# A sixth first-layer tile by three products, and other homes for the turned keys, queries and guards

## The chip, the cores and the metric

One core of a Trainium2 chip runs the whole kernel. TensorE (PE) multiplies matrices, and its weight loads are listed apart as PEld. VectorE (DVE) and ScalarE (ACT) work element by element, GpSimd (POOL) issues some DMAs here, and SyncE (SP) issues most of them. Each engine works through its own list of instructions. The metric is the device time of one execution in microseconds (us).

## The reference

A gated linear attention over 768 steps, in 4 batches of 8 heads with 48 columns, and behind it a two-layer network over the 3,072 rows that come out, with the activation h·cos(h):

```python
mag = np.sqrt(a_re * a_re + a_im * a_im)
scale = np.minimum(mag, 0.999) / (mag + 1e-06)
a_re_n, a_im_n = (a_re * scale, a_im * scale)
for t in range(S):
    new_re = ar * S_re - ai * S_im
    new_im = ar * S_im + ai * S_re
    kv = np.einsum('bhd,bhe->bhde', k[:, :, t], v[:, :, t])
    S_re, S_im = (new_re + kv, new_im)
    y[:, :, t] = np.einsum('bhd,bhde->bhe', q[:, :, t], S_re)
x = np.ascontiguousarray(y.transpose(0, 2, 1, 3)).reshape(B * S, H * D)
h = x @ w_in            # 384 -> 2048
g = h * np.cos(h)
return (g @ w_out).astype(np.float32)   # 2048 -> 384
```

## The kernel before

The 3,072 rows are cut into 24 chunks of 128 steps, and two chunks make a group, so there are 12 groups, numbered 0 to 11. Three groups make a batch. Groups 0 and 1 are written out by hand. From group 2 on a loop over n builds three things in one turn: the attention of group n (scores `sc`, the causal mask that gives `atm`, the values `yp`, and the state `sp` carried on), the gates of group n + 1 (logarithms `lg`, exponentials, angles `tan`, then the keys `ks` and queries `qs` with their factors), and the two layers. The second layer of group n − 1 (`op`, `sum`, seven products in place of eight) is threaded through the attention of group n, and the first layer of group n (`hp`) closes the turn. On PE a turn is therefore: scores and values of the group's two chunks between second-layer products, the sums `lgs` and `phs` of the next group's gates, the rest of the second layer, and the first layer. The seam between two turns is where the first layer of group n ends and the scores of group n + 1 start.

The first layer has 8 tiles of 256 columns. A plain tile is six matmuls in full float32, and the profile lists each as two records of 128x256. From a certain group on (table `FROM`) a tile runs by three products instead: x and the weights are cut into an upper and a lower part (`xh`, `xl`, `wh`, `wl`) and a combination of them (`xx`, `wx`), and three times six matmuls in the rounded format give `hp` (two of the products, summed in PSUM) and `hb` (the third). ACT copies `hb` out of PSUM, and DVE adds it to `hp` ahead of the gate. `halves` converts a tile's weights once, at the end of group `FROM` − 1, and `x_halves` cuts x in each group: DVE makes `cut`, `xl`, `xx`, and ACT copies `xh`.

Each gate is a sine and a square on ACT and a product on DVE. Each `hp` takes one PSUM bank, from homes that rotate.

Keys and queries have to stand with their columns on the partitions. `f_transpose` turns them in blocks on DVE (a transpose of 128x1536 into `tr`), SP stores the turned blocks to DRAM (`moved`) and loads them back as `kT` (four loads) and `qT` (one). The attention's output `yT` goes to DRAM and back as `xT` in the same way. SP's list is one queue: a DMA that waits holds the ones behind it.

The weights come as 64-bit numbers. `guard` loads a raw piece again (POOL's DMA) and lets ACT look at its exponents in two passes; two pieces a group, for groups 3 to 10.

The order is set in three ways. PE's list is written out: each matmul is chained behind the one before it, in the order in which `weave` sorts the parts by the numbers beside them. ACT's table functions are chained too. The other rows of DVE and ACT are placed by the framework's scheduler, under the dependencies of tiles and those added by `behind`.

## Time and profile before

| what | us |
|---|---|
| median of three runs | 637.14 |
| lowest and highest of them | 637.04, 642.63 |
| the profiled execution | 635.72 |
| span of its trace, first to last instruction | 633.8 |
| PE idle in this span | 10.4 |
| DVE busy | 530.4 |
| ACT busy | 450.2 |

The span is shorter than the execution by what lies ahead of the first instruction and behind the last. PE's idle time is the span less its busy time of 623.4 us, and nearly half of it is the end, where the last sums are stored. A matmul's duration includes its way through the array, so that records of 0.37 us follow each other in shorter steps: how long a tile takes is read from the starts of the rows. In the rows of the timeline, "x36" is a count of equal records in a row, and what stands in brackets is idle time of the engine ahead of the row and who ended it.

### The profile page before, as it was taken

What the parts mean: (1) busy time and instruction counts of PE and PEld (TensorE: products, weight loads), DVE (VectorE), ACT (ScalarE), POOL (GpSimd) and SP (SyncE); (2) the same over time, 40 slices, a digit from 0 to 9 for tenths busy, and PEclk for the clock granted to TensorE, in tenths of its full rate; (3) what the DMA queues carried; (4) which work ended last, traced back from release to release, by engine and by line L of the source; (5) the groups of instructions that cost most, each with busy time, mean ns of one, the idle gap of its engine ahead of it and who ended that gap; (6) DMA issues with size and microseconds to landing.
All of it is one profiled execution on the core that took longest, in us unless ns stands there. A gap on an engine that the chain in (4) does not pass through costs nothing.

```text
span 633.8 us, 11436 instructions
## 1 busy us (share of the span) xinstructions
PE 623.4 (98%) x4321; PEld 571.4 (90%) x4321; DVE 530.4 (84%) x856; ACT 450.2 (71%) x812; POOL 30.2 (5%) x53
## 2 busy tenths in 40 slices
PE   8999999999999999999999999999999999999996
PEld 6788967677899899999999999999999999999996
DVE  6999989868698799899888998988988988983371
ACT  7888688286597598599598598599598598562350
POOL 4010110000000000000000000000000000000000
PEclk9999999999999999999999999999999999999999
DMA  9968564715926855765865775685675583361001
GB/s 227 254 192 225 177 195 79 199 55 116 243 63 149 215 135 146 180 175 126 201 175 132 180 189 126 172 189 139 177 185 138 162 179 135 111 140 51 26 2 31
DMA packets 232923, 94.94 MB, mean 150 GB/s; under 512 B 208701, under 2 KB 221246, under 8 KB 232858
## 3 DMA queue, kind: packets, MB, share of 16 engines
q1 hardware_dynamic: 225320, 68.51, 47.1%
q0 software_dynamic: 5824, 25.50, 12.1%
q8 instruction: 36, 0.59, 0.4%
q10 hardware_dynamic: 1714, 0.11, 0.2%
q14 instruction: 29, 0.24, 0.1%
HBM read 69.28 MB, written 24.81 MB: 148 GB/s over the span
## 4 chain that ended last, share of the span: by engine, by line
PE 92%; ACT 3%; DVE 3%; issue 1%; DMA 1%; SPq 0%; DVEq 0%
PE hp L692 30%; PE op L692 19%; PE sum L692 16%; PE sc L692 7%; PE yp L692 6%; PE hb L692 5%; PE sp L692 4%; PE phs L692 2%; PE lgs L692 2%; PE yr L692 1%; PE tp L1006 1%; DMA im<-in_a_im_dram 1%; ACT tan L712 1%; DVE tan L681 0%; ACT lg L712 0%
## 5 line engine op out<-in xcount | busy, mean ns | idle before, releaser
L692 PE MATMUL hp<-xT,w_in 128*128 128x256 f32 (+1 forms) x684 | 146.9, 372 | 0.7 <-DVE gate L681 0.7
L692 PEld LDWEIGHTS hp<-xT,w_in 128*128 128x128 f32 x684 | 125.9, 190 | 18.5 <-DVE gate L681 1.1
L692 PE MATMUL op<-w_out,gate 128*128 128x192 f32 (+1 forms) x464 | 103.2, 372 | 0.0
L712 ACT ACTIVATE gate<-hp,half_pi_b 128x512 f32<-128x512 f32 x96 | 65.9, 687 | 43.8 <-PE hp L692 40.4
L692 PEld LDWEIGHTS op<-w_out,gate 128*128 128x128 f32 x464 | 78.7, 190 | 16.7 <-issue 1.9
L681 ACT ACTIVATE junk<-hp 128x512 bf16<-128x512 f32 x96 | 57.2, 596 | 0.0
L692 PE MATMUL sum<-w_out,gate 128*128 128x192 f32 x304 | 54.6, 328 | 0.0
L681 DVE TENSOR_TENSOR gate<-hp,gate 128x512 f32<-128x512 f32 x55 | 37.6, 685 | 18.4 <-ACT junk L681 17.7
L692 PEld LDWEIGHTS sum<-w_out,gate 128*128 128x128 f32 x304 | 49.2, 190 | 0.0
L692 PE MATMUL sc<-qT,kT 96*128 96x128 f32 x384 | 48.9, 276 | 0.3 <-ACT qT L681 0.3
L692 PEld LDWEIGHTS sc<-qT,kT 96*128 96x128 f32 x384 | 46.8, 192 | 2.0 <-issue 0.6
L692 PE MATMUL hp<-xh,wh 128*128 128x256 f32 x246 | 44.2, 288 | 0.0
L692 PE MATMUL hp<-xl,wl 128*128 128x256 f32 x246 | 42.5, 281 | 0.0
L681 DVE TENSOR_TENSOR hp<-hp,gate 128x512 f32<-128x512 f32 x41 | 28.6, 698 | 16.5 <-PE hp L692 7.0
L681 DVE TENSOR_TENSOR atm<-sc,causal 128x512 f32<-128x512 f32 x48 | 32.6, 684 | 7.2 <-PE sc L692 7.2
L681 ACT ACTIVATE ot<-sum 128x192 f32<-128x192 f32 x39 | 12.7, 325 | 34.9 <-PE sum L692 34.9
L681 ACT COPY yT<-yp 48x512 f32<-48x512 f32 x44 | 25.4, 577 | 16.5 <-PE yp L692 16.0
L692 PEld LDWEIGHTS hp<-xh,wh 128*128 128x128 f32 x246 | 35.8, 189 | 0.5
L692 PE MATMUL hb<-xx,wx 128*128 128x256 f32 x246 | 35.1, 284 | 0.0
L681 ACT ACTIVATE gate<-hb 128x512 f32<-128x512 f32 x41 | 24.5, 599 | 14.7 <-PE hb L692 14.0
L692 PEld LDWEIGHTS hp<-xl,wl 128*128 128x128 f32 x246 | 34.8, 188 | 0.0
L681 DVE TENSOR_TENSOR gate<-gate 128x256 f32<-128x256 f32 x80 | 32.2, 417 | 3.0 <-PE op L692 2.5
(163 smaller groups left out, 1275.2 us busy)
## 6 DMA issues: line engine op xcount, KB each, us to landing
moved<-tr SPq DMA_DIRECT2D x20, 768.0 KB
raw<-in_moe_w_in_dram POOLq DMA_DIRECT2D x16, 768.0 KB, 5.5
raw<-in_moe_w_out_dram POOLq DMA_DIRECT2D x16, 768.0 KB, 4.9
kT<-moved SPq DMA_DIRECT2D x40, 192.0 KB
qT<-moved SPq DMA_DIRECT2D x10, 768.0 KB
k<-in_k_dram SPq DMA_DIRECT2D x24, 192.0 KB
q<-in_q_dram SPq DMA_DIRECT2D x24, 192.0 KB
v<-in_v_dram SPq DMA_DIRECT2D x24, 192.0 KB
```

What stands on the lines that cost most here:

```text
L681: ins = getattr(self.engine, op)(**kw)
L692: chain(nc.tensor.matmul(out, **kw), "tensor")
L712: chain(nc.scalar.activation(func=func, **kw))
L1006: chain(nc.tensor.transpose(ps[:, h], X[g][name[0] + "s"][:, x0 + h].rearrange("p a d -> p (a d)"), ident), "tensor")
```

## The change

It has five parts.

1. `FROM` gets a sixth tile, 2, from group 5 on, and tiles 3 and 6 start one group earlier. Tiles by three products: 2 before and 3 now in group 3, 4 and 5 in group 4, 5 and 6 from group 5 on, that is 41 and 50 in all. The conversions lie in groups 2 (three), 3 (two) and 4 (one), in place of two, two and one.
2. The turned keys lie in `kT`'s own home and the turned queries in `qT`'s, ahead of the loads that fill these. Before, they had the home `tr` and the home of `pair`.
3. The guards' raw pieces, which had `tr`'s home, lie in the homes of `kT` and `qT` too, once the attention of the group has read these. Their places in the turn are 0.47 and 0.505 instead of 0.26 and 0.47, and the small copy on POOL that held them back is gone.
4. x is halved between the two turns. `cut` comes behind the keys' turn, `xl` and `xx` follow, and the queries' turn is placed behind `xx`. Before, both turns came first.
5. The store of x goes ahead of the load of `im` in SP's queue. And `hp` rotates over four banks from group 2 on, in place of three.

```diff
-    def guard(src):
-        _, e = fetched(src)
+    def guard(src, home):
+        _, e = fetched(src, home)
...
     def f_transpose(g, i, n, name):
-        if i == 0:
-            X[g][name] = ft.tile([D2, G * H, Q4, 32] if name == "kT" else [D2, Q4, G * H, 32], F32,
-                                 tag=name, name=name, bufs=1)
-        pool, tag = (ft, "tr") if name == "kT" else (gt, "pair")
-        tr = pool.tile([C, NB, n * H, 32], F32, tag=tag, name="tr", bufs=1)
+        tr = ft.tile([C, NB, n * H, 32], F32, tag=name, name="tr", bufs=1)
...
         X[g][name + " turn"] = turn
+        if g and name == AHEAD and "apart" in X[g - 1]:
+            behind(turn, X[g - 1]["apart"])
...
+        X[g][name] = ft.tile([D2, G * H, Q4, 32] if name == "kT" else [D2, Q4, G * H, 32], F32,
+                             tag=name, name=name, bufs=1)
...
-            home = "mmc"[len(order) % 3] if g != 1 else "a"
+            home = "a" if g == 1 else "mamc"[len(order) % 4] if g else "mmc"[len(order) % 3]
...
-            vector.tensor_scalar(out=x["cut"].bitcast(U32), in0=whole.bitcast(U32), scalar1=UPPER,
-                                 scalar2=None, op0=ALU.bitwise_and)
+            cut_ = vector.tensor_scalar(out=x["cut"].bitcast(U32), in0=whole.bitcast(U32), scalar1=UPPER,
+                                        scalar2=None, op0=ALU.bitwise_and)
+            if g + 1 < NG:
+                behind(cut_, X[g + 1][BEFORE])
...
-            copied = scalar.copy(out=x["xh"], in_=x["cut"])
-            if g + 1 < NG:
-                behind(copied, x["square"])
-            low = vector.tensor_tensor(out=x["xl"], in0=all_of(), in1=x["cut"], op=ALU.subtract)
-            if g + 1 < NG:
-                behind(low, X[g + 1]["qT turn"])
-                behind(low, x["product"])
+            scalar.copy(out=x["xh"], in_=x["cut"])
+            vector.tensor_tensor(out=x["xl"], in0=all_of(), in1=x["cut"], op=ALU.subtract)
...
+        if "apart" in x and g + 1 < NG and jp == x["order"][0]:
+            behind(gated, x["apart"])
...
-    FROM, UPPER, SHIFT = {3: 5, 4: 3, 5: 3, 6: 4, 7: 4}, 0xFFFFF000, 4096.0
+    FROM, UPPER, SHIFT = {2: 5, 3: 4, 4: 3, 5: 3, 6: 3, 7: 4}, 0xFFFFF000, 4096.0
+    BEFORE, AHEAD = "kT turn", "qT"
...
-            yield lambda: load(g + 1, ("re", "im"))
+            yield lambda: load(g + 1, ("re",))
...
-        yield lambda: (f_x(g), f_xt(g))
+        yield lambda: (f_x(g), g + 2 < NG and load(g + 2, ("im",), put=after_x), f_xt(g))
...
-              (convert[0:1], 0.82, 0.82), (convert[1:2], 0.93, 0.93),
+              (convert[0:-2], 0.76, 0.76), (convert[-2:], 0.76, 0.98),
```

In the lists of the engines this shows at three places, all taken from the turn that ends at the seam of 370.66 us in the trace of before. The first is DVE behind the gates, where keys and queries are turned and x is halved (`end` is a small step of the state). Before:

```order
L681 STREAM_TRANSPOSE tr_3182<-ks_3165 128x1536
L681 STREAM_TRANSPOSE tr_3203<-qs_3166 128x1536
L681 TENSOR_SCALAR cut_3171<-xT_3081 128x768
L681 TENSOR_TENSOR gate_3197<-hp_3190,gate_3197 128x512
L681 TENSOR_TENSOR xl_3169<-xT_3081,cut_3171 128x768
L681 SCALAR_TENSOR_TENSOR xx_3168<-xl_3169,cut_3171 128x768
L681 TENSOR_SCALAR end_3063<-end_3063 96x16
```

The same place on DVE now:

```order
L681 STREAM_TRANSPOSE tr_3224<-ks_3213 128x1536
L681 TENSOR_SCALAR cut_3236<-xT_3125 128x768
L681 TENSOR_TENSOR xl_3234<-xT_3125,cut_3236 128x768
L681 SCALAR_TENSOR_TENSOR xx_3233<-xl_3234,cut_3236 128x768
L681 TENSOR_TENSOR gate_3248<-hp_3241,gate_3248 128x512
L681 STREAM_TRANSPOSE tr_3253<-qs_3214 128x1536
L681 TENSOR_SCALAR end_3101<-end_3101 96x16
```

The three steps of x and the first gate have moved ahead of the queries' turn.

The second place is SP's queue behind the turns: the stores of the turned blocks (`moved`), the loads of `kT` and `qT`, and what stands behind them. Before:

```order
L990 DMA moved_3184<-tr_3182 128x1536
L990 DMA moved_3205<-tr_3203 128x1536
L994 DMA kT_3181<-moved_3184 96x16x32 x4
L996 DMA qT_3202<-moved_3205 96x4x512
L1488 DMA out_0_dram<-ot_2939 128x384
L1488 DMA out_0_dram<-ot_2938 128x384
L1488 DMA k_3210<-in_k_dram 128x8x48 x2
```

SP's queue at the same place now:

```order
L988 DMA moved_3226<-tr_3224 128x1536
L994 DMA kT_3228<-moved_3226 96x16x32 x4
L988 DMA moved_3255<-tr_3253 128x1536
L996 DMA qT_3257<-moved_3255 96x4x512
L1493 DMA out_0_dram<-ot_2988 128x384
L1493 DMA out_0_dram<-ot_2987 128x384
L1493 DMA k_3261<-in_k_dram 128x8x48 x2
```

The four loads of `kT` now stand ahead of the store of the queries.

The third place is DVE at the seam: the masks `atm` of the first chunk's scores, the logarithm steps of the next gates (`lg`, `pair`), the last gates, and the mixes of gates for the second layer (`s`, and `gate` from gates). Before:

```order
L681 TENSOR_TENSOR atm_3405<-sc_3406,causal_165 128x512
L681 TENSOR_TENSOR lg_3378<-lg_3378,tan_3379 128x768
L681 TENSOR_TENSOR s_3412<-gate_3240,gate_3342 128x256
L681 SCALAR_TENSOR_TENSOR gate_3371<-hp_3351,gate_3371 128x512
L681 TENSOR_TENSOR atm_3405<-sc_3421,causal_165 128x512
L681 TENSOR_TENSOR s_3427<-gate_3265,gate_3371 128x256
L681 SCALAR_TENSOR_TENSOR state_3439<-sp_3430,state_3018 96x384
L681 TENSOR_TENSOR gate_3240<-gate_3240 128x2x128
L681 TENSOR_TENSOR state_3439<-state_3439,end_3063 96x384
L681 SCALAR_TENSOR_TENSOR pair_3381<-re_3031,pair_3381 128x768
L681 TENSOR_SCALAR lg_3378<-lg_3378 128x768
```

DVE at the same seam now:

```order
L681 TENSOR_TENSOR lg_3441<-lg_3441,tan_3442 128x768
L681 TENSOR_TENSOR gate_3301<-gate_3301 128x2x128
L681 SCALAR_TENSOR_TENSOR gate_3434<-hp_3414,gate_3434 128x512
L681 TENSOR_TENSOR s_3490<-gate_3324,gate_3434 128x256
L681 TENSOR_TENSOR gate_3324<-gate_3324 128x2x128
L681 SCALAR_TENSOR_TENSOR pair_3444<-re_3075,pair_3444 128x768
L681 TENSOR_SCALAR lg_3441<-lg_3441 128x768
L681 TENSOR_TENSOR atm_3468<-sc_3469,causal_165 128x512
L681 TENSOR_TENSOR lg_3441<-lg_3441,rs_3443 128x768
L681 TENSOR_TENSOR gate_3248<-s_3412,gate_3248 128x2x128
L681 TENSOR_TENSOR gate_3276<-s_3452,gate_3276 128x2x128
L681 TENSOR_TENSOR atm_3468<-sc_3484,causal_165 128x512
```

The first mask has moved from ahead of the logarithm steps to behind `pair` and `lg<-lg`, and the second to behind `lg<-lg,rs`. The seams ahead of groups 6 to 10 have this form now, two of them (groups 6 and 9) with one mix fewer ahead of the second mask. At the seam ahead of group 4 the first mask stands ahead of `pair` and the second behind `lg<-lg,rs`; at that of group 5 the second mask stands right behind `lg<-lg`; at those of groups 3 and 11 both stand ahead of these steps. PE's list is the same as before, but for the nine tiles.

More of the change, by code (lines that the diff above doesn't have):

```diff
@@ L1509, in wait_for, with guarded @@
         chain(nc.gpsimd.tensor_copy(out=after, in_=tile), "gpsimd")
-    def guarded(g, count):
-        if guards:
-            yield lambda: wait_for(X[g]["gate"][X[g]["order"][-1]][0:1, 0, 0:1])
-        for _ in range(min(count, len(guards))):
-            yield lambda: guard(guards.pop(0))
+    def guarded(homes):
+        for home, _ in zip(homes, list(guards)):
+            yield lambda home=home: guard(guards.pop(0), home)
     into, back = weight_parts()
     guards = [src for _, src in into + back if src.dtype != F32]
-    per = -(-len(guards) // (NG - 3))
     after = consts.tile([1, 1], F32, name="after")
@@ L1800, in fast_path @@
         split = x_halves(n) if any(three(n, jp) for jp in THREE) else ()
-        guard_ = list(guarded(n - 1, per)) if n > 2 else []
+        guard_ = list(guarded(("kT", "qT"))) if n > 2 else []
         convert = [lambda jp=jp: halves(jp) for jp in THREE if FROM[jp] == n + 1]
-        if split and n < NG - 1:
-            X[n + 1]["upper"] = split[0]
         weave((mixes(n - 1, 2, 4), 0.0, 0.08), (logs(n + 1), 0.0, 0.02), (chunks(n), 0.0, 0.36),
```

24 lines of the change are left out of this document (14 added, 10 removed).

## Prediction

> **What bounds the kernel now.** I read the page's busy times first, then the windows by loop turn, and then the timelines of PE, DVE, ACT and SP around one seam between two turns of the loop over groups (all rows that follow show the start and the duration in us).
>
> The page, then two windows (busy time of PE, PEld, DVE, ACT and POOL, granted clock, DMA share, GB/s):
>
> ```profile
> PE 623.4 (98%) x4321; PEld 571.4 (90%) x4321; DVE 530.4 (84%) x856; ACT 450.2 (71%) x812; POOL 30.2 (5%) x53
> ...
> 322.40:370.70 48.30, 48.30 (x363) 46.43 (x362) 42.99 (x69) 37.65 (x70) 1.67 (x3) 1.00 0.67 164
> 630.00:634.00 4.00, 0.00 (x0) 0.00 (x0) 0.00 (x0) 0.00 (x0) 0.00 (x0) 0.71 0.12 35
> ```
>
> PE sets the time: in a turn of 48.3 us it is busy for all 48.3. A shorter matmul stream is a direct gain, but every new wait of PE is a direct loss, since PE has no idle time to take it from. DVE, at 43.0 of 48.3 us, is the engine that can make PE wait.
>
> One seam on PE (start, duration): the end of the first layer of one group, then the chunks of the next.
>
> ```profile
> 352.19 7.93 PE L692 MATMUL hp<-xT,w_in 128*128 128x256 f32 x36
> 359.77 0.70 PE L692 MATMUL hp<-xh,wh 128*128 128x256 f32 x3
> ...
> 367.09 0.52 PE L692 MATMUL hp<-xh,wh 128*128 128x256 f32 x3
> ...
> 369.23 0.51 PE L692 MATMUL hp<-xh,wh 128*128 128x256 f32 x3
> ...
> 370.66 1.05 PE L692 MATMUL sc<-qT,kT 96*128 96x128 f32 x8
> ...
> 375.06 1.53 PE L692 MATMUL sum<-w_out,gate 128*128 128x192 f32 x8
> 376.52 0.43 PE L692 MATMUL yp<-atm,v 128*48 128x128 f32 x4
> ...
> 377.44 0.39 PE L692 MATMUL yp<-atm,v 128*48 128x128 f32 x4
> ...
> 378.42 1.57 PE L692 MATMUL op<-w_out,gate 128*128 128x192 f32 x8
> ```
>
> Call 370.66, where the scores `sc` start, the seam's zero. The values `yp` of the first chunk start at 5.86; their first four heads need the first mask `atm`, the last four (377.44, at 6.78) the second. The same seam on DVE and ACT:
>
> ```profile
> 372.13 0.68 DVE L681 TENSOR_TENSOR atm<-sc,causal 128x512 f32<-128x512 f32 x1
> 372.74 0.96 DVE L681 TENSOR_TENSOR lg<-lg,tan 128x768 f32<-128x768 f32 x1
> ...
> 374.55 0.68 DVE L681 TENSOR_TENSOR atm<-sc,causal 128x512 f32<-128x512 f32 x1
> ...
> 377.02 0.96 DVE L681 SCALAR_TENSOR_TENSOR pair<-re,pair 128x768 f32<-128x768 f32 x1 [0.19 <-ACT pair L712]
> 377.89 0.55 DVE L681 TENSOR_SCALAR lg<-lg 128x768 f32<-128x768 f32 x1
> 378.36 0.42 DVE L681 TENSOR_TENSOR gate<-gate 128x256 f32<-128x256 f32 x1
> 378.79 0.96 DVE L681 TENSOR_TENSOR lg<-lg,rs 128x768 f32<-128x768 f32 x1
> 379.67 1.08 DVE L681 TENSOR_TENSOR gate<-s,gate 128x256 f32<-128x256 f32 x3
> ...
> 373.88 1.28 ACT L708 ACT_TABLE_LOAD   x1
> ...
> 376.89 0.83 ACT L712 ACTIVATE rs<-lg 128x768 f32<-128x768 f32 x1
> ...
> 377.84 0.93 ACT L712 ACTIVATE rs<-rs,one_b 128x768 f32<-128x768 f32 x1
> ```
>
> Both masks are done at 375.23, 1.3 us before `yp`. The logarithm steps come after them: `pair` waits for ACT's exponential, which stands behind the last gate and a table load of 1.28 us. In this order that wait (0.19 us) costs nothing.
>
> **The sixth tile.** A plain tile takes 12 records: three of them take 359.77 − 352.19 = 7.58 us, so 2.53 each. A tile by three products takes 369.23 − 367.09 = 2.14. The first such tile costs 0.18 more (0.70 against 0.52), as before. Nine tiles change form (one in group 3, one in group 4, one in each of groups 5 to 11): 9 × 0.39 = 3.5 us off PE. What the form adds beside PE, per tile one more ACT step out of PSUM and one DVE sum, lies in the first layer, where both engines wait for PE. The one conversion more (now three in group 2) lies beside plain tiles of 2.53 us. I cost both at nothing; where ACT falls behind, the logarithms of the seam come later, up to about one step (0.8 us) a seam.
>
> **The fourth home for `hp`.** In group 2, PE waits once for a bank:
>
> ```profile
> 162.01 13.22 PE L692 MATMUL hp<-xT,w_in 128*128 128x256 f32 x60 [0.67 <-DVE gate L681]
> ```
>
> With four homes the fifth tile needs the first gate later, so 0.7 us goes. Sum so far: −4.2.
>
> **Halving x between the turns.** The turns of keys and queries on DVE, the halving of x behind them, and SP's queue after the turns:
>
> ```profile
> 353.67 2.25 DVE L681 STREAM_TRANSPOSE tr<-ks 128x1536 f32<-128x1536 f32 x1
> 355.86 2.20 DVE L681 STREAM_TRANSPOSE tr<-qs 128x1536 f32<-128x1536 f32 x1
> 357.98 0.52 DVE L681 TENSOR_SCALAR cut<-xT 128x768 uint32<-128x768 uint32 x1
> ...
> 359.02 0.94 DVE L681 TENSOR_TENSOR xl<-xT,cut 128x768 fp32r<-128x768 f32 x1
> 359.99 0.96 DVE L681 SCALAR_TENSOR_TENSOR xx<-xl,cut 128x768 fp32r<-128x768 f32 x1
> ...
> 354.98 0.69 ACT L712 ACTIVATE gate<-hp,half_pi_b 128x512 f32<-128x512 f32 x1 [2.26 <-PE hp L692]
> ...
> 358.58 0.83 ACT L681 CAST xh<-cut 128x768 fp32r<-128x768 f32 x1 [2.33 <-DVE cut L681]
> ...
> 355.95 2.48 SPq L990 DMA_DIRECT2D moved<-tr  x2
> 359.16 4.20 SPq L994 DMA_DIRECT2D kT<-moved  x4
> 363.47 1.10 SPq L996 DMA_DIRECT2D qT<-moved  x1
> ```
>
> The tiles by three products now start after two plain ones, at 352.19 + 5.06 = 357.25. The keys' turn frees DVE at 355.9 (the queries' turn starts 2.19 after it); `cut`, `xl`, `xx` then end near 356.4, 357.3 and 358.2. The copy `xh` on ACT (0.83) can be there at about 357.2, just in time; `xl` is needed three matmuls, `xx` twelve matmuls later. I take 0, with 0.3 us a turn (some 2 us in all) as the upper end.
>
> **Turned keys, queries and guards.** The guards' two passes on ACT keep one place and take another in the 2.3 us in which ACT waits for the first tile, so nothing; if they landed late, the keys' turn on DVE, and all behind it, would wait for them. SP now issues the keys' four loads ahead of the queries' store. Before, store to landing took at most 359.16 − 355.95 = 3.2 us, and `qT` had 370.66 − 363.47 = 7.2 us to land. Now: loads until 363.4, store 3.2, and at most 7.2 for the load, so 373.8 at the latest against scores wanted at 370.3. The likely landing is near 370, as the store alone took 3.2 for the same bytes. Scores later by up to 3.5 us are covered where the masks are later still (next part), and cost up to 3.5 us elsewhere. I take 0. `x` ahead of `im` brings xT earlier; PE does not wait for xT now, so 0.
>
> **The masks' place on DVE.** This decides. As the order in the section on the change shows, at this seam the two masks now stand behind `pair` and `lg<-lg`, and the second also behind `lg<-lg,rs` and two mixes. The chain on ACT does not move: it hangs on the last gate. So DVE reaches the first mask at 378.36 (where the mix stood) and ends it at 379.04; `lg<-lg,rs` from 378.97 takes 0.88, two mixes 0.34 each, and the second mask runs from 380.52 to 381.20. `yp` starts 2.5 us late, and its second half at 381.25 instead of 377.44: 3.8 us. All that PE has after it shifts; the second chunk's masks fit under the shifted work (by my count to within 0.3 us), and nothing later in the turn had idle time to give back. Where the change puts one mix fewer ahead of the second mask, the first chunk of a batch is at hand, whose halves are shorter:
>
> ```profile
> 328.28 1.08 PE L692 MATMUL yp<-atm,v 128*48 128x128 f32 x16
> 330.55 0.96 DVE L681 TENSOR_TENSOR lg<-lg,rs 128x768 f32<-128x768 f32 x1
> ...
> 231.72 0.39 PE L692 MATMUL yp<-atm,v 128*48 128x128 f32 x4
> 235.09 0.96 DVE L681 TENSOR_TENSOR lg<-lg,rs 128x768 f32<-128x768 f32 x1
> ...
> 281.60 0.39 PE L692 MATMUL yp<-atm,v 128*48 128x128 f32 x4
> 282.76 0.55 DVE L681 TENSOR_SCALAR lg<-lg 128x768 f32<-128x768 f32 x1
> ```
>
> There the first mask again goes ahead of `lg<-lg,rs`: 330.7 + 0.88 + 0.34 + 0.68 = 332.6 against the second half at 328.8, so 3.8 too. Five seams (chunks of groups 6 to 10) have these forms: 19. At group 4's only the second mask is behind: 235.09 + 0.88 + 0.68 = 236.65 against 231.72, so 4.9. At group 5's it is behind `lg<-lg` alone: 282.76 + 0.47 + 0.68 = 283.9 against 281.60, so 2.3. Groups 3 and 11 have both masks ahead of such waits: 0.2 at most. Sum: 19 + 4.9 + 2.3 + 0.2 = 26.4.
>
> The seam leaves PE idle for 2.5 and then 1.3 us, at group 4's for 4.9 at one stretch. In the profile the clock is 1.00 in all turns, and 0.71 in the last four microseconds, with PE idle. The Trainium skill (TensorE: Matmul & The Clock Gate, section "What's actually happening", the table of the two states) says that a whole idle window of about 3.4 us halves the clock until PE has been busy for another such window. By it the sum would, as an estimate, be 1.7 us longer, for the one gap that can hold a window; the last row fits it, and no gap before that is long enough to test it.
>
> **Sum.** 26.4 − 4.2 = +22.2 us on the profiled execution's 635.7, so 657.9. The median of the runs, 637.14, is 1.4 above that execution; on it the sum is 659.3. I say 659.
>
> **Rivals.**
> 1. Not slower: PE doesn't lose at the masks, because something else ends the wait, or the work after `yp` catches up. What speaks for it is only that nothing waits there now. Then the gain stands alone: 637.1 − 4.2 = 632.9, 0.7% down. It decides if `yp` starts under 0.5 us late at each of seven seams. Against it: DVE's rows of the trace stand in the order of the program. Chance 0.06.
> 2. The queries land late as well: up to 3.5 us at the seams that the masks don't cover (group 11, 3.5; group 3, whose turns are earlier, some 2; group 5, 1.2): +6.7, so 666. Chance 0.12.
> 3. Only the first mask counts, since ACT's chain or the mixes are quicker: 2.5 instead of 3.8 at five seams, so 653. Chance 0.08.
> 4. The clock falls in each of the seven gaps: at half clock the rest of `yp` (377.44 to 378.42) and the `op` behind it (1.57) cost up to 2.6 us more, so up to 18 in all, 677. Every gap but one is split by half a `yp`. Chance 0.06.
>
> **How the numbers follow.** The forecast has 0.68, the rivals 0.32. The range 651 to 668 takes in the forecast, rival 2 and rival 3 with the 2 us of `xh`, which makes 0.86, less some 0.05 for what I don't see. One per cent is about what a measurement here can tell from no change: faster by over 1% means under 630.8, below even rival 1, so 0.01; within 1%, 0.05; slower, 0.94.
>
> **What would show it.** Right: PE rows of `yp<-atm` in groups 6 to 10 with an idle time before them released by DVE's `atm`, about 2.5 and 1.3 us; PE's idle time up by 26; `hp<-xT` down by 108 records, each of the three product groups up by 54. Wrong: no such idle time, or `sc` waiting for a DMA, or a clock below 1.00 in these windows.

## The result, and the profile after

| what | before | after |
|---|---|---|
| median, us | 637.64 | 692.40 |
| lowest and highest, us | 637.04, 642.63 | 690.92, 695.37 |
| the profiled execution, us | 635.72 | 690.92 |
| span of its trace, us | 633.8 | 689.1 |
| PE busy, us | 623.4 | 639.8 |
| PE idle in the span, us | 10.4 | 49.3 |
| mean granted clock of PE | 0.998 | 0.965 |

The changed kernel is slower by 8.5%: the ratio is 1.0846, with a 95% interval of 1.0779 to 1.0913. The prediction had the direction. Its time of 659.0 and its range up to 668 fell short.

The span grew by 55.3 us, in two parts that the table shows. PE is idle for 38.9 us more. And it is busy for 16.4 us more, although nine tiles went to the shorter form (3.5 us less by the prediction's rows): some 19.9 us are matmuls at a lower clock.

PE's waits after (total us, how many, the longest), the costliest first:

```profile
PE sc L692 <- DMA qT<-moved: 17.6, 4, 4.8
PE sum L692 <- DVE gate L681: 10.5, 4, 4.3
PE sc L692 <- issue: 5.5, 2, 4.5
PE sc L692 <- ACT tan L756: 3.7, 1, 3.7
PE sc L692 <- ACT junk L681: 3.1, 1, 3.1
```

Four of these rows are one thing. The scores wait at eight of the nine seams from group 3 on, 29.9 us in all. Where the row names that load, the wait ends 5.9 to 6.3 us after its issue; where the row names ACT or nothing, it ends 5.9 to 7.0 us after it, so it is taken for the same wait. The other row is new in kind: `sum`, the first product of the second layer, waits for a gate of the first layer.

One steady seam on PE (the one ahead of group 7): start of the first layer, its end, and the chunk behind it.

```profile
375.36 5.34 PE L692 MATMUL hp<-xT,w_in 128*128 128x256 f32 x24
...
393.02 0.52 PE L692 MATMUL hp<-xl,wl 128*128 128x256 f32 x3
398.27 2.05 PE L692 MATMUL sc<-qT,kT 96*128 96x128 f32 x8 [4.73 <-DMA qT<-moved]
400.11 2.77 PE L692 MATMUL sum<-w_out,gate 128*128 128x192 f32 x8
...
406.42 0.43 PE L692 MATMUL yp<-atm,v 128*48 128x128 f32 x4
```

Before, eight score records took 1.05 us and eight of `sum` 1.53; here 2.05 and 2.77. The first values `yp` start 8.15 us after the scores, not 5.86: 2.3 us go to the clock, on top of 4.73 of waiting. `yp` itself doesn't wait, so the masks, on which the prediction rested, cost nothing here. The clock in three stretches of this seam (column PEclk, the third from the end):

```profile
393.00:398.20 5.20, 0.54 (x5) 0.34 (x3) 5.03 (x11) 5.17 (x10) 0.00 (x0) 0.79 0.89 234
398.20:401.50 3.30, 3.23 (x13) 3.26 (x14) 1.99 (x4) 3.24 (x5) 0.00 (x0) 0.50 1.14 225
401.50:405.00 3.50, 3.50 (x30) 3.50 (x28) 3.00 (x6) 3.00 (x5) 0.00 (x0) 0.81 0.02 4
```

And the queue of SP ahead of this seam:

```profile
379.11 0.34 SPq L988 DMA_DIRECT2D moved<-tr  x1
382.44 4.10 SPq L994 DMA_DIRECT2D kT<-moved  x4
386.63 2.36 SPq L988 DMA_DIRECT2D moved<-tr  x1
392.35 0.33 SPq L996 DMA_DIRECT2D qT<-moved  x1
```

On DVE, the queries' turn, for which the second store waits:

```profile
382.03 2.29 DVE L681 STREAM_TRANSPOSE tr<-qs 128x1536 f32<-128x1536 f32 x1
```

The queries' turn ends at 384.32, but SP is still issuing the keys' loads, so the store goes out at 386.63. From there to the load's issue pass 5.7 us (3.2 in the prediction), and from that issue to the scores 5.9. This order of the queue holds at seven of the nine seams, ahead of groups 5 to 11; from the store to the load's issue it is 4.3 to 5.7 us there, so the seam shown is the longest.

### The profile page after: what moved, and what is told of

It reads as the page before. It is cut to its first block, busy times and chain, and to the rows that moved or that the text cites. A ratio compares the mean times of both kernels' runs of the same rounds, so it can differ in the third digit from the quotient of the medians.

```text
span 689.1 us, 11622 instructions
## 1 busy us (share of the span) xinstructions
PE 639.8 (93%) x4375; PEld 588.8 (85%) x4375; DVE 543.5 (79%) x868; ACT 457.7 (66%) x823; POOL 28.3 (4%) x45
## 4 chain that ended last, share of the span: by engine, by line
PE 76%; DVE 8%; ACT 7%; DMA 6%; issue 2%; SPq 0%; ACTq 0%; DVEq 0%
PE hp L692 18%; PE op L692 18%; PE sum L692 16%; PE sc L692 7%; PE yp L692 6%; PE sp L692 4%; DMA qT<-moved 3%; PE hb L692 2%; PE phs L692 2%; ACT gate L712 2%; DVE gate L681 2%; DVE tr L681 2%; DMA moved<-tr 2%; ACT junk L681 1%; PE lgs L692 1%
## 5 line engine op out<-in xcount | busy, mean ns | idle before, releaser
L692 PE MATMUL hp<-xT,w_in 128*128 128x256 f32 (+1 forms) x576 | 123.1, 371 | 0.0
L692 PEld LDWEIGHTS hp<-xT,w_in 128*128 128x128 f32 x576 | 105.6, 190 | 14.7 <-issue 0.2
L692 PEld LDWEIGHTS sc<-qT,kT 96*128 96x128 f32 x384 | 53.8, 215 | 33.1 <-issue 20.5
L692 PE MATMUL sum<-w_out,gate 128*128 128x192 f32 x304 | 67.0, 378 | 10.5 <-DVE gate L681 10.5
L692 PEld LDWEIGHTS sum<-w_out,gate 128*128 128x128 f32 x304 | 60.1, 225 | 11.2 <-issue 10.4
L692 PE MATMUL hp<-xh,wh 128*128 128x256 f32 x300 | 53.2, 286 | 0.0
L692 PE MATMUL hp<-xl,wl 128*128 128x256 f32 x300 | 51.7, 281 | 0.0
L692 PEld LDWEIGHTS hp<-xh,wh 128*128 128x128 f32 x300 | 43.2, 189 | 0.9 <-ACT xh L681 0.5
L692 PE MATMUL hb<-xx,wx 128*128 128x256 f32 x300 | 42.8, 283 | 0.0
L692 PEld LDWEIGHTS hp<-xl,wl 128*128 128x128 f32 x300 | 42.5, 188 | 0.0
L681 DVE SCALAR_TENSOR_TENSOR gate<-hp,gate 128x512 f32<-128x512 f32 x50 | 34.3, 686 | 8.8 <-ACT junk L681 8.7
```

Source lines behind the costliest of these rows:

```text
L681: ins = getattr(self.engine, op)(**kw)
L692: chain(nc.tensor.matmul(out, **kw), "tensor")
```

## The experiments

Fifteen kernels ran in five groups, each beside runs of the kernel before, whose medians there were 636.7 to 637.2. Times below are medians, and the ratio to before stands with its interval.

### The homes of `hp`

The first group set two theories of the trace against the prediction's masks. The fourth home: the rotation "mamc" puts the eighth tile into c, the one bank of the tag `acc`, which the next turn's `sum` takes too. The queue: the queries land late. The changed kernel with three homes again:

```diff
-            home = "a" if g == 1 else "mamc"[len(order) % 4] if g else "mmc"[len(order) % 3]
+            home = "a" if g == 1 else "mmc"[len(order) % 3]
```

> The changed kernel with the three homes of before for hp, all else as changed. Three theories are on trial. Queue: the queries' store stands behind the keys' four loads in SP's queue, so the queries land 4 to 5 us late, and PE's clock falls in the gap. Home: with four homes the eighth tile lies in the bank that the next group's sum takes, so sum waits for the last gate. Masks: what the prediction said. The home theory expects the waits of sum for gate (10.5 us in four of them, in the seams ahead of groups 3, 4 and 5 and at the end) to go to below 1 us, and the time to fall by about 10, to some 682. The queue theory alone expects the waits of sc in the steady seams to stay at 4 to 5 us each, whatever the homes. If the home were behind the late scores too (they take banks of the same pool as the fourth home), those waits would go as well, and the time would be near 655.

Measured: 665.65, ratio 1.0452 (1.0432 to 1.0473), 27 us below the changed kernel rather than 10. `sum` no longer waits at all. The scores wait 15.4 us in all instead of 29.9, and a wait of `hp` for the first gate appears:

```profile
PE sc L692 <- ACT gate L712: 7.6, 3, 2.7
PE hp L692 <- DVE gate L681: 7.0, 8, 1.4
PE sc L692 <- ACT junk L681: 4.7, 2, 2.8
PE sc L692 <- DMA qT<-moved: 3.1, 2, 1.6
```

The kernel before with the fourth home alone:

```diff
-            home = "mmc"[len(order) % 3] if g != 1 else "a"
+            home = "a" if g == 1 else "mamc"[len(order) % 4] if g else "mmc"[len(order) % 3]
```

> The kernel before with the fourth home for hp alone (four homes in the order of the change from group 2 on). Home: sum waits for the last gate at every seam, by up to 3 us, so 10 to 30 us longer than before, 648 to 668. The prediction's term (0.7 us shorter): 637. Queue: no effect on the queries, no wait of sc for a DMA.

Measured: 688.59, ratio 1.0829 (1.0771 to 1.0886). This one line takes the kernel before to almost the time of the whole change, and beyond the 648 to 668 that I had expected of it. The first row of its waits, then one seam on PE and on DVE:

```profile
PE sum L692 <- DVE gate L681: 30.9, 10, 5.0
```

```profile
394.44 1.05 PE L692 MATMUL sc<-qT,kT 96*128 96x128 f32 x8
398.82 2.19 PE L692 MATMUL sum<-w_out,gate 128*128 128x192 f32 x8 [3.33 <-DVE gate L681]
```

```profile
397.99 0.68 DVE L681 SCALAR_TENSOR_TENSOR gate<-hp,gate 128x512 f32<-128x512 f32 x1
```

The scores start at once, since the queries are on time. Then `sum` starts 0.15 us after the end of the last gate (397.99 + 0.68 = 398.67): that product is the last reader of the eighth tile, and it stands behind the whole chain of the tile on ACT and DVE. Of the 49.5 us that the span grew (683.3 against 633.8), 30.9 are this wait and 18.9 are PE's busy time (642.3 against 623.4), that is the clock.

To see whether a fourth home or its place is at fault, the changed kernel with the banks in another order, so that the third tile lies in c:

```diff
-            home = "a" if g == 1 else "mamc"[len(order) % 4] if g else "mmc"[len(order) % 3]
+            home = "a" if g == 1 else "macmmamm"[len(order)] if g else "mmc"[len(order) % 3]
```

> The changed kernel with another rotation of the four kinds of bank: the first layer's tiles lie in m, a, c, m, m, a, m, m, so that the bank of sum (c) holds the third tile and is free long before the seam. Home: no wait of sum for a gate (below 1 us in all), as with three homes, and no wait of hp for a gate either (6.3 us in the steady turns with three homes). Queue: the queries land when they did, so what hp no longer waits for is added to the wait of sc, 2.5 to 4.7 us at each of seven seams, and the time is 655 to 670, near the one with three homes. If the queries were late only because hp waited, or the home were the only fault, the time would be 633.

Measured: 668.27, ratio 1.0469 (1.0425 to 1.0513), as expected of the two theories together. Neither `sum` nor `hp` waits. The scores wait 23.8 us (the rows of `sc` summed), up to 3.6 at a seam. The two costliest of these rows:

```profile
PE sc L692 <- DMA qT<-moved: 12.6, 4, 3.6
PE sc L692 <- ACT junk L681: 6.4, 2, 3.2
```

So it is the place: the same number of banks, 24 us less. And what the bank gave back to `hp` (7.0 us) went to the wait of the scores.

A run with one line changed can differ from its neighbour in more than that line. The lists of SP and DVE aren't written out as PE's is, and they moved with the homes. In the two runs with other homes (665.65 and 668.27) both stores stand ahead of the keys' loads, and on DVE the queries' turn stands ahead of the first gate, at all seams from group 6 on but the last. SP in the run at 668.27, ahead of group 7:

```profile
364.79 4.99 SPq L988 DMA_DIRECT2D moved<-tr  x2
369.95 6.34 SPq L994 DMA_DIRECT2D kT<-moved  x4
```

The gain of 24 us is therefore that of the bank together with these orders. That the bank by itself makes `sum` wait is what the run at 688.59 shows.

### The late queries

The order of SP's queue was the first suspect. The changed kernel with the keys' loads behind the queries' store, as before:

```diff
         if name == "kT":
-            for q4 in range(Q4):
-                nc.sync.dma_start(out=X[g][name][:, ds(i * H, n * H), q4], in_=moved[q4])
+            X[g]["kT loads"] = [(X[g][name][:, ds(i * H, n * H), q4], moved[q4]) for q4 in range(Q4)]
         else:
+            for home, src in X[g].pop("kT loads"):
+                behind(nc.sync.dma_start(out=home, in_=src), put)
             late["qT"] = nc.sync.dma_start(out=X[g][name][:, :, ds(i * H, n * H)],
```

> The changed kernel with the keys' four loads issued behind the queries' store, the order of SP's queue before; the turns on DVE and all else stay as changed. Queue: the queries' store lands 3.2 us after its issue in place of 5.7, the queries' load is issued some 3 us earlier, the scores wait about 2 us at a steady seam instead of 4 to 5, the gap is below 3.4 us and the clock of PE stays at full speed (eight score records in 1.05 us, not 2.05): 7 seams with 2.5 to 3 less of waiting and 2.3 less of slow matmuls, so some 36 us less, near 657. Masks: as soon as the queries are on time, the waits of yp for atm appear (2.5 and 1.3 us a seam), and the time stays above 670. Home: the waits of sum for gate stay (10.5) and appear at the steady seams also, up to 3 us each.

Measured: 697.83, ratio 1.0937 (1.0908 to 1.0966): no gain. The queries are as late as in the changed kernel, only for another reason:

```profile
383.09 4.99 SPq L988 DMA_DIRECT2D moved<-tr  x2
388.24 6.38 SPq L996 DMA_DIRECT2D kT<-moved  x4
394.79 0.96 SPq L997 DMA_DIRECT2D qT<-moved  x1
```

```profile
402.02 2.05 PE L692 MATMUL sc<-qT,kT 96*128 96x128 f32 x8 [4.51 <-DMA qT<-moved]
```

The keys' turn ends at 383.06. Its loads could start some 3 us later, but stand behind a store that waits for the queries' turn (385.40 to 387.70). The theory in its first form, that the order in the list is the fault, fell. What stays is that the queries' turn comes late, and that one list then has two orders to choose from, both bad. This run has the order that the two runs with other homes got by themselves, and the queries' load goes out as late as in the run at 668.27, some 15.4 us after the start of the first layer.

The changed kernel with both turns first, the halving of x behind them:

```diff
-    BEFORE, AHEAD = "kT turn", "qT"
+    BEFORE, AHEAD = "qT turn", None
...
-              (split[0:1], *[0.57 if n < NG - 1 else 0.525] * 2),
+              (split[0:1], *[0.601 if n < NG - 1 else 0.525] * 2),
```

(and 0.602 and 0.603 for the other two steps). Once with the homes of the change, once with those of the last run:

> The changed kernel with both turns ahead of the halving of x, as before, so that SP's queue has its order of before; six tiles by three products, four homes, and all else as changed. Queue: no late queries (waits of sc below 1 us in all), but the first tile by three products starts after two plain tiles, before xh is there: about 2.2 us a turn in seven turns, 15 in all. With the home's waits of 10 to 30 us the time would be 660 to 680; without them (home theory wrong) some 650. Masks: yp waits for atm by 2 to 4 us a seam on top of that.

> The changed kernel with both turns ahead of the halving of x and with the rotation m, a, c, m, m, a, m, m; six tiles. Home and queue: no wait of sum for a gate, none of sc for the queries; only the first tile by three products waits for xh, 2.0 to 2.5 us in each of six turns (12.8 in all with the four homes of the change), so 637 - 4 + 13 = 646. Sixth tile as a cost of its own (its added steps on ACT and DVE): 655 or more. Masks: where they stand behind the logarithms on DVE, 2.6 and 0.3 us of waiting for each such seam come on top.

With "mamc": 708.02, ratio 1.1102 (1.1059 to 1.1146). The queries are on time, so the whole price of the bank shows: `sum` waits 33.1 us, `hp` waits 12.8 for `xh`. That is beyond what I expected, since the clock falls at most seams as well. With the other homes: 646.25, ratio 1.0154 (1.0139 to 1.0168), which is what the sum gave. Nearly all that is left is the wait for `xh` (`yp` waits 0.8 us for masks, `sc` 0.7):

```profile
PE hp L692 <- ACT xh L681: 11.0, 6, 2.5
```

The sixth tile thus has its price on either side: with two plain tiles ahead, x is halved either too late for PE (11.0 us) or ahead of the queries' turn.

What the halving between the turns costs without a sixth tile and without a fourth home:

```diff
-    FROM, UPPER, SHIFT = {2: 5, 3: 4, 4: 3, 5: 3, 6: 3, 7: 4}, 0xFFFFF000, 4096.0
+    FROM, UPPER, SHIFT = {3: 5, 4: 3, 5: 3, 6: 4, 7: 4}, 0xFFFFF000, 4096.0
...
+            home = "a" if g == 1 else "mmc"[len(order) % 3]
```

> The changed kernel with the five tiles by three products and the three homes of before; x is still halved between the turns of keys and queries. Queue: the sixth tile only shortens the first layer by 0.4 us a turn, so the scores still wait for the queries at the steady seams, about 2 us each, with the clock falling at some: 650 to 660. If the sixth tile's shorter first layer (or its added steps on ACT and DVE) is what makes the queries late, the time is that of before, 637.

> As the run with five tiles and three homes, but with both turns ahead of the halving of x: what is left of the change are the turned keys, queries and guards in the homes of kT and qT, the store of x ahead of im, and the places of the conversions. Queue and home: nothing of it costs, 636 to 639, no wait of PE of over 1 us in the loop. If the homes of the turned blocks or the guards delay the turns, the scores wait for the queries here too, 645 or more.

Halving between the turns: 657.43, ratio 1.0313 (1.0274 to 1.0352). Both turns first: 646.58, ratio 1.0146 (1.0114 to 1.0178). The 11 us between them are late queries: the scores wait 7.7 us in the one and not in the other, and at the last seam the clock falls too. In both runs `hp` waits for the first gate, 8.3 and 8.8 us. The waits of the first:

```profile
PE hp L692 <- DVE gate L681: 8.3, 8, 1.5
PE sc L692 <- ACT junk L681: 3.6, 2, 2.9
PE sc L692 <- DMA qT<-moved: 2.7, 4, 1.0
...
PE sc L692 <- issue: 1.4, 1, 1.4
```

The second run isn't the kernel before in time, as I had expected. Its 9.4 us are the wait of `hp`: with three homes the fourth tile takes the first tile's bank and waits for that tile's gate, and this gate had become late. Two places could make it so. On ACT, the copy `xh` stood ahead of the gate's sine; on DVE, `xx` stood ahead of the gate's product. Two lines that the change drops had kept these apart. One came back first, then both:

```diff
-            scalar.copy(out=x["xh"], in_=x["cut"])
-            vector.tensor_tensor(out=x["xl"], in0=all_of(), in1=x["cut"], op=ALU.subtract)
+            copied = scalar.copy(out=x["xh"], in_=x["cut"])
+            if g + 1 < NG:
+                behind(copied, x["square"])
+            low = vector.tensor_tensor(out=x["xl"], in0=all_of(), in1=x["cut"], op=ALU.subtract)
+            if g + 1 < NG:
+                behind(low, x["product"])
```

(the first of the two runs without the last two lines and `low`).

> The run with five tiles, three homes and both turns first (646.6) had hp wait 8.8 us for the first gate. In its trace ACT's copy xh stands ahead of the first gate and waits about 5 us for cut, which stands behind the turns on DVE. Here the line that the change drops is back: xh is held behind the first tile's square. If this place of the copy is the cause, the wait of hp falls to 0.7 us (the one in group 2) and the time to that of before, 637. If the first gate is late for another reason (its place on DVE behind xx), hp still waits over 5 us and the time stays at 645 or more.

> The last run with five tiles, three homes and both turns first, with the second line that the change drops back as well: xl is held behind the first tile's product on DVE, so that the first gate stands ahead of xl and xx again. If this place on DVE is what makes hp wait (in the run without it the sine on ACT is done some 5 us before the product starts, which stands behind xx), the waits of hp fall from 8.9 us to 0.7 and the time to 637, that of the kernel before. If they stay, the cause is elsewhere, and the time stays at 646.

With the line on ACT: 646.56, ratio 1.0156 (1.0136 to 1.0176), no change. With both: 637.11, ratio 1.0018 (0.9987 to 1.0049), the time of before. The first of these on ACT and on DVE:

```profile
359.33 0.69 ACT L712 ACTIVATE gate<-hp,half_pi_b 128x512 f32<-128x512 f32 x1 [1.46 <-PE hp L692]
```

```profile
363.93 0.96 DVE L681 SCALAR_TENSOR_TENSOR xx<-xl,cut 128x768 fp32r<-128x768 f32 x1
...
365.09 1.88 DVE L681 TENSOR_TENSOR gate<-hp,gate 128x512 f32<-128x512 f32 x3
```

The sine is done at 360.0, and the product starts 5.1 us later, behind `xx`. That is the place. In the change this price is hidden by the fourth home, which lets the fourth tile start without that gate.

Last, the queries' store from ACT's list, with the homes of the run at 668.27, so that in SP's queue no store that waits for the queries' turn holds back the keys' loads:

```diff
-        put = nc.sync.dma_start(out=moved.rearrange("q (r b) x j -> (q r) b x j", b=NB), in_=tr)
+        queue = nc.scalar if name == "qT" and g > PEG + 1 else nc.sync
+        put = queue.dma_start(out=moved.rearrange("q (r b) x j -> (q r) b x j", b=NB), in_=tr)
```

> The changed kernel with the rotation m, a, c, m, m, a, m, m, and the queries' store issued from ACT's list in place of SP's, so that it neither stands behind the keys' four loads nor they behind it. Queue, in its first form (the order in SP's list makes the queries late): the queries' load is issued some 2.5 us earlier, the wait of sc falls from 2.7 to 3.6 to about 1 us a seam, below what lowers the clock, and the time falls from 668 to some 645. Second form (the transfers themselves, above all the keys' loads in pieces of 128 bytes, keep the DMA engines busy, so the queries land late in any order once their turn comes 2.4 us later): no gain, 660 to 670.

Measured: 648.53, ratio 1.0203 (1.0158 to 1.0247): 20 us less than with the store in SP's list. The store leaves 0.03 us after the turn, and the load follows 4.6 us later:

```profile
362.39 2.29 DVE L681 STREAM_TRANSPOSE tr<-qs 128x1536 f32<-128x1536 f32 x1
...
364.71 0.33 ACTq L989 DMA_DIRECT2D moved<-tr  x1
...
369.33 0.71 SPq L997 DMA_DIRECT2D qT<-moved  x1
```

So one queue for both was the larger part of the delay. The rest is the later turn: seven waits of `sc` of 0.6 to 2.0 are left (8.7 us), and ACT, which now waits for the turn itself ahead of the first gate, makes `hp` wait 4.4 us.

The same with `xh` behind the first square again, and the steps of x emitted behind the first tile (places 0.59, 0.592 and 0.594):

> The run with the queries' store on ACT's list (648.5) with the same line back, so that the first gate goes ahead of xh; the steps of x are emitted behind the first tile. Six tiles, homes m, a, c, m, m, a, m, m. If hp's 4.4 us of waiting only move to the scores, which wait for the queries anyway, the time stays at 644 to 649. If the earlier gates also let the queries' turn and its store go earlier, it falls to 640 or below, and with the 4.2 us of shorter matmuls it could come under the kernel before.

Measured: 660.03, ratio 1.0361 (1.0331 to 1.0391), worse. `hp` waits 13.3 us for `xh` in three turns, up to 5.4 at once. In the one shown the store stands ahead of the first gate and of `xh` in ACT's list, and ACT does nothing for 7.4 us: the store goes out at 370.08, when the queries' turn on DVE has ended (370.05). The row names `least`, a small step of DVE right behind that turn:

```profile
370.08 0.33 ACTq L989 DMA_DIRECT2D moved<-tr  x1
370.45 0.69 ACT L712 ACTIVATE gate<-hp,half_pi_b 128x512 f32<-128x512 f32 x1 [7.36 <-DVE least L681]
...
371.61 0.83 ACT L681 CAST xh<-cut 128x768 fp32r<-128x768 f32 x1
```

Whether the waits of `hp` and of `sc` are in parallel this run doesn't tell; a store that waits for its data holds what stands behind it in its list, the gates on ACT as the keys' loads on SP.

The seam ahead of group 7 in five kernels, in us from the start of that turn's first layer:

| kernel | queries' turn ends | their load is issued | scores start |
|---|---|---|---|
| before | 5.9 | 11.3 | 18.5 |
| changed | 9.0 | 17.0 | 22.9 |
| five tiles, three homes | 8.4 | 13.6 | 21.2 |
| six tiles, homes m, a, c, m, m, a, m, m | 8.4 | 15.4 | 21.7 |
| the same, store from ACT's list | 8.4 | 13.0 | 20.0 |

### The clock

The changed kernel with ten matmuls that nobody reads in the gap, ahead of the scores of groups 6 to 11:

```diff
-        return [lambda jp=jp: mm1(g, jp, jp == order[-1]) for jp in order]
+        return [lambda jp=jp: (mm1(g, jp, jp == order[-1]),
+                               jp == order[-1] and 4 < g < NG - 1 and fill(10)) for jp in order]
+
+    def fill(count):
+        ps = pa.tile([C, 512], F32, tag="a", name="busy")
+        for _ in range(count):
+            matmul(ps[:, 0:E2], lhsT=w_out[:, 0, 0:C], rhs=w_out[:, 1, 0:E2],
+                   start=True, stop=True)
```

> The changed kernel with ten matmuls of 128x192 (some 3.3 us, their result is read by nobody) on PE behind the last first-layer tile of groups 5 to 10, where PE otherwise waits for the queries. Clock: PE is busy through most of the gap, so the first eight score records take 1.05 to 1.15 us again in place of 2.05, and the eight of sum 1.5 in place of 2.8, some 2.2 us at each of six seams: 679. If the slow matmuls behind the gap have another cause (the transfers that run beside them, say), they stay slow and the time stays at 692 or grows.

Measured: 674.87, ratio 1.0602 (1.0581 to 1.0624): 17.5 us shorter than the changed kernel, by adding work. The same seam:

```profile
389.05 3.41 PE L692 MATMUL busy<-w_out 128*128 128x192 f32 x20
393.21 1.13 PE L692 MATMUL sc<-qT,kT 96*128 96x128 f32 x8 [0.75 <-DMA qT<-moved]
394.18 1.47 PE L692 MATMUL sum<-w_out,gate 128*128 128x192 f32 x8
```

The scores start hardly earlier (22.2 us after the start of the first layer, 22.9 in the changed kernel), but they and `sum` run at full speed. PE's busy time is 644.4, of which 6 × 3.41 = 20.5 are the filling: 623.9 of real work against 639.8, so 15.9 us less. At the six filled seams the way from the first score to the first `yp` is 5.94 us each time, where it took 5.94 to 8.48 in the changed kernel: 11.1 us less in all. The remainder lies mostly where nothing was filled, at the seam ahead of group 3 and at the last sums, where the clock fell in the one run and not, or less, in the other.

### The prediction's masks

The kernel before, with the first chunk's masks of groups 6 to 10 put where the change has them:

```diff
+        if 6 <= g <= 10 and i == 0:
+            behind(y["masked"], X[g + 1][("halved", "less")[hh]])
```

(`halved` is the step `lg<-lg`, `less` the step `lg<-lg,rs`).

> The kernel before with the first chunk's masks of groups 6 to 10 held behind the logarithm steps of the next group on DVE, as the change places them (the first behind the halving of lg, the second behind lg less rs). The prediction's price: yp waits 2.5 us for the first mask and 1.3 for the second, 3.8 at each of five seams, 656. If the price was wrong, and the work behind covers the masks: 637 to 641. With the clock falling in a gap of 2.5 us (as behind the waits of sum and sc): up to 667.

Measured: 661.30, ratio 1.0371 (1.0336 to 1.0406). The price exists. The sum of the waits, and one of the five seams:

```profile
PE yp L692 <- DVE atm L681: 14.6, 11, 2.6
```

```profile
384.65 0.43 PE L692 MATMUL yp<-atm,v 128*48 128x128 f32 x4 [2.60 <-DVE atm L681]
386.02 0.42 PE L692 MATMUL yp<-atm,v 128*48 128x128 f32 x4 [0.29 <-DVE atm L681]
```

The first mask is late by 2.6 us (2.5 in the prediction), the second by 0.3 more and not 1.3. Of that 1.0 us, 0.7 is the edit's: it holds the second mask behind `lg<-lg,rs`, but the two mixes of 0.34 that stood between them in the prediction's count went ahead of `pair` here. The span grew by 21.2 us: 14.3 of these waits (14.6 less the 0.3 that the kernel before has too), 4.8 of PE's busy time (628.2 against 623.4), where the clock falls, and 1.5 of waits of `sc`.

The second mask's place follows the bank. In the kernel before with the fourth home alone, nothing of the other parts of the change is there, and the second mask stands behind `lg<-lg` all the same. In the changed kernel with three homes both masks stand ahead of `pair`, as before. DVE in the two, at the seam ahead of group 7:

```profile
402.26 0.55 DVE L681 TENSOR_SCALAR lg<-lg 128x768 f32<-128x768 f32 x1
402.76 0.69 DVE L681 TENSOR_TENSOR atm<-sc,causal 128x512 f32<-128x512 f32 x1
```

```profile
385.51 0.68 DVE L681 TENSOR_TENSOR atm<-sc,causal 128x512 f32<-128x512 f32 x1
...
387.89 0.95 DVE L681 SCALAR_TENSOR_TENSOR pair<-re,pair 128x768 f32<-128x768 f32 x1
```

It is so in every kernel here but the one above that forces the order: where the eighth tile lies in c, the second mask of groups 6 to 10 comes behind `lg<-lg`; where it doesn't, both come ahead of `pair`. PE's list offers a reason, since `sum` stands between the two halves of the scores, so a late `sum` makes the second half late. That the scheduler moved the mask for this reason was not tried. The first mask stands behind `pair` in the changed kernel alone, and why is open.

### What is left of the change without its costs

The sixth tile in group 11 only, where no turn follows, tiles 3 and 6 a group earlier as in the change, both turns first, and the homes "macmmamm":

```diff
-    FROM, UPPER, SHIFT = {2: 5, 3: 4, 4: 3, 5: 3, 6: 3, 7: 4}, 0xFFFFF000, 4096.0
+    FROM, UPPER, SHIFT = {2: 11, 3: 4, 4: 3, 5: 3, 6: 3, 7: 4}, 0xFFFFF000, 4096.0
```

> The changed kernel with what has been shown to cost taken out: the sixth tile goes by three products from group 11 on only (no turn follows there), tiles 3 and 6 start a group earlier as in the change, both turns stand ahead of the halving of x, and the homes rotate m, a, c, m, m, a, m, m. Three tiles more than before by three products: 3 x 0.39 = 1.2 us less, and 0.7 for the bank in group 2: 635, if nothing else of the change costs. If the turned blocks' homes, the guards or the order of x and im cost, it is above 640.

Measured: 636.39 against 636.77 in the same group, ratio 0.9997 (0.9968 to 1.0025): no difference that can be measured; the 1.9 us expected lie inside the interval. The turned blocks' homes, the guards, the places of the conversions and the store of x ahead of `im` therefore have no cost that shows here. By the upper end of the interval (1.6 us above before) and the gain of 1.9, they cost at most some 3.5 us together. This version doesn't beat the kernel before; none of the fifteen did.

## Why the prediction was right in direction and wrong in size

The direction was right for a reason that didn't act, and that is luck. The prediction had 26.4 us from the masks, which cost nothing in the changed kernel. The 54.8 us that were measured come from terms that it took at −0.7 (the fourth home) and at 0 (the queries, the halving of x), with the clock behind their waits.

**The fourth home.** "With four homes the fifth tile needs the first gate later, so 0.7 us goes." This is the step that failed most. The gain is there (the row of 0.67 us is gone), but I followed the rotation to the fifth tile and stopped. Its eighth letter is c, and c is the bank of the next turn's `sum`. Alone it costs 51.6 us (688.59 − 636.97).

**The queries.** "I take 0", with 3.5 us as the upper bound, and the masks as cover. The 0 rests on 3.2 us for the store and as much again for the load, by their bytes: 363.4 + 3.2 + 3.2 is near 370. The store behind the keys' loads took 5.7 us and the load 5.9. With these the count gives 369.1 for the load's issue, 375.0 for the landing, and scores wanted at 370.3: 4.7 late. The trace has 4.73 at this seam; that it agrees so closely is chance, as the other six stores in this place took 4.3 to 5.6. The bound of 3.5 failed by the store, since 7.2 for the load was ample. The cover was argued the wrong way round: a wait that comes earlier in the seam hides the later one. In the changed kernel the masks disappeared behind the scores' wait.

**The masks.** "This decides." The price was nearly right where it was tried by itself: 19 us predicted for five seams, 24 measured, 14.3 of them the waits themselves. But in the changed kernel it decided nothing: `yp` waits for a mask once, 0.3 us. The order on DVE was read rightly, and it wasn't on the path. And the second mask's place came with the bank, the term that stood at −0.7: among the kernels here, only the forced one has this mask behind `lg<-lg` while both `sum` and the scores are on time.

**Halving x between the turns.** "I take 0", with some 2 us as the upper end. I looked at when `xh` is there for PE, and that held: no more than 0.5 us of waiting. What I didn't follow is the queries' turn behind these steps. The runs give 11 us for it (657.43 against 646.58), and 9.4 for the first gate behind `xx` on DVE, where there are only three homes (646.58 against 637.11 with both lines back).

**The clock.** The prediction gave it 1.7 us in the sentence on the Trainium skill, and a rival of 18 us a chance of 0.06. It took about 19.9 us. The price was as the rival put it, but the gaps were other ones: not at the masks, but ahead of the scores or of `sum`.

**The sixth tile.** A tile by three products takes 2.14 us again in the changed kernel (383.40 to 385.54), and three tiles more in the last run took 1.5 us off PE's busy time (621.9 against 623.4) where 1.2 was to be expected. The full 3.5 us for nine tiles doesn't show: in the run with both turns first and the bank mended PE is busy for 621.3 us, 2.1 less than before, with six waits for `xh` in it. How much of the difference these waits make is not separated. In the changed kernel the time saved goes into the wait of the scores. Between five and six tiles with three homes the time even rises, from 657.43 to 665.65, as the scores wait 7.7 us more. The load of the queries lands up to 0.7 us later there; why wasn't tried.

One sum in the prediction is off: the chances of the forecast, rival 2 and rival 3 add up to 0.88, not 0.86.

How the two faults add up: the late queries and the late first gate cost 28.7 us without the fourth home (665.65), the fourth home 51.6 without them (688.59), and both together 54.8. At a steady seam they are parallel. `sum` couldn't start before some 4.4 us after the end of the first layer (398.82 against 394.44 in the run with the home alone), and the late scores start 4.7 us after it. Whoever mends only one sees little: 668 with the bank mended, and with the queries on time but the bank as it is 708, 12.8 of it waits for `xh`.

## What to carry to other kernels

When a rotation of buffers is widened, write out which home the last element gets and who takes that home next: the wait that it removes is at the front, the one that it makes is at the end. A step that is put between two transfers of one chain is to be charged to the second transfer, with the queue in which that one then stands, not only to its own reader. Waits that start at the same point of a stage hide each other: the predicted one can be right by itself and worth nothing. And where a scheduler places the rows, ask which part of the change moved them before an order is priced as a cause.

## What the runs showed of the hardware

The lower clock comes with gaps much shorter than I had taken from the profile of before. In the run with the store on ACT's list a gap of 2.00 us was enough, in the run with the bank c mended one of 2.97 was not:

```profile
427.93 2.05 PE L692 MATMUL sc<-qT,kT 96*128 96x128 f32 x8 [2.00 <-ACT tan L756]
```

```profile
277.60 1.13 PE L692 MATMUL sc<-qT,kT 96*128 96x128 f32 x8 [2.97 <-ACT lg L756]
```

The Trainium skill (TensorE: Matmul & The Clock Gate, section "What's actually happening") says that the clock halves after a whole idle window of about 3.4 us, and that the window runs free of the kernel. The second half of this agrees with the scatter seen here, and the granted 0.50 with the halving; the gap of 2.00 us doesn't agree with a whole idle window. In these runs gaps of 2.0 to 3.7 us were followed by the lower clock in some cases and not in others (after one of 3.70 ahead of group 5 in the changed kernel eight score records took 1.13 us). Those of over 4.2 us ahead of the scores were followed by it in all seven cases, at the seam shown above for some 4.5 us from the scores on.

A store of 768 KB that stood right behind the keys' four loads took 5.7 us to land (4.3 to 5.7 over seven seams), where the keys' store ahead of them took 3.3 (379.11 to 382.44; 3.3 to 3.8). The loads were issued until 386.54, so the store ran beside their tail. That the tail is what slows it was not tried by itself.
